# Mixing one chunk of tokens with matrix products, and a new order for the first stage of a banded-attention and gated feed-forward kernel

## The chip, the cores and the metric

The kernel runs on one core of one Trainium2 chip. The metric is device time in microseconds (us), the median over several executions; lower is better. TensorE (PE) does matrix products, with its weight loads (PEld) shown apart; VectorE is DVE, ScalarE is ACT, GpSimd is POOL, and SP is the engine that issues all transfers (DMA).

## The reference

Eight batches, eight heads, 576 tokens, 64 numbers per head, all fp32. Per head, two attentions are added. The pooled one averages q, k and v over groups of four tokens (144 groups), attends over all groups, and repeats each result four times. The local one attends only to tokens less than four away.

```python
out_up = np.repeat(sm_attn(q_d, k_d, v_d), 4, axis=2)      # q_d, k_d, v_d: means over 4 tokens
scores = np.where(np.abs(pos[:, None] - pos[None, :]) < 4, scale * q @ k.T, -1e9)
x = out_up + softmax(scores) @ v                            # heads side by side: (8, 576, 512)
x_prev = x shifted by one token, zeros in front
xk = mu_k * x + (1 - mu_k) * x_prev
xr = mu_r * x + (1 - mu_r) * x_prev
v  = np.maximum(xk @ w_k, 0) ** 2 @ w_v                     # w_k 512x1024, w_v 1024x512
out = sigmoid(xr @ w_r) * v                                 # w_r 512x512
```

The weights w_k, w_v, w_r arrive in double precision.

## The kernel before

**Attention.** Two heads make a pair; a batch has four pairs, and there are 32 of them (`n`). For a pair, q and k are loaded in 128-byte pieces (`load_raw`), turned on VectorE, and pooled on GpSimd. v is loaded twice: pooled groups (`load_v4`) and windows of 32 tokens (`load_windows`). The scores go to PSUM; `score_*` is the local softmax, `down_*` the pooled one. `down_turn` transposes the pooled probabilities with TensorE, in two tiles that share the 144 keys: keys 0 to 111 in one, keys 16 to 143 in the other, of which 80 to 143 are used. `av_pe` multiplies with v. Its pooled product has two halves (64 columns of sums per head, on array rows 0 to 63 and 64 to 127), and the second tile is added in a second step on rows 64 to 127. The result is `xts[b]`, x turned so that features lie on partitions.

**Feed-forward.** The 4608 tokens are cut into 18 chunks of 256 (`c`). Mixing makes xk and xr. Since x*mu + x_prev*(1-mu) is x_prev + mu*(x - x_prev), chunk 0 and 1 take the difference on GpSimd (`diff`), scale it on ScalarE (`mix_part`), and add on VectorE (`mix_add`); `mix_high` rounds to the faster format fp32r, and `mix_low` keeps what is left. Every product is made of three such products: high by high, high by low, low by high. `k_pe` is the first layer, `v_pe` the second, `r_pe` the gate, `store_mul` and `store_out` the end.

**Weights.** Twenty blocks (k0 to k7, v0 to v7, r0 to r3) of 512 KB each. A block is fetched, scaled on ScalarE, put together from its two integer words in three passes on VectorE, and split into high and low parts; the low part of the first eight (in the order of `WORDER`) is made by two products on TensorE (`weight_diff`), of the others by GpSimd. It needs a PSUM bank from its scaling on.

**Order.** All work is written as tasks with an engine, a cost, a rank, and the tiles that they read and write. `Plan.order` places one task after another: the one that can start first on its engine, and among those that can start at that time the one with the lowest rank. This order is fixed for every engine's queue. `SHIFT` is a table of additions to ranks, for tasks of chunks 0 to 3, pairs 0 to 9 and the weights. Six PSUM banks are handed out by the plan, and two more hold scores. Where TensorE would be idle during the first 100 us of the plan, `fill` puts in products whose results nobody reads (`keep_warm`). The lines that the rows name: L281 and L282 load the mixing's coefficients; L320 fetches a weight block; L325 to L360 convert it; L356 is filler; L600 to L602 are `down_turn`; L620, L624 and L630 are `av_pe`; L664 writes x; L685 to L719 are the mixing; L727 is `k_pe` of chunks 0 and 1; L792 is `v_pe`; L796 multiplies by the gate.

Of the kernel before, what the change touches and what calls it, by code (L numbers as in the profile page):

```python
# [16 lines left out]
DM, DFF = 512, 1024  # L17
# [22 lines left out]
KA = 112  # L40
SHIFT = {
# [24 lines left out]
class Plan:  # L66
# [18 lines left out]
    def shift(self, name, args):  # L85
        if not args:
            return SHIFT.get(name, 0.0)
        i, more = args[0], args[1:]
# [166 lines left out]
def attention_moe(ctx: ExitStack, tc, q, k, v, mu_k, mu_r, w_k, w_v, w_r, band, ident, out):  # L255
# [10 lines left out]
    muk = cp.tile([P, NP], F32, name="muk")  # L266
    mur = cp.tile([P, NP], F32, name="mur")
# [34 lines left out]
    raws, ws, shaped, part32 = {}, {}, {}, {}  # L302

# [78 lines left out]
    def load_v4(n):  # L382
        b, p = divmod(n, NP)
        v4 = v4s[n % 2]
        base = (b * H + 2 * p) * S * D
        nc.sync.dma_start(v4[0:KA, 0:2, :], bass.AP(v.tensor, base, [[4 * D, KA], [S * D, 2], [1, 4 * D]]))
        nc.sync.dma_start(v4[96:P, 2:4, :], bass.AP(v.tensor, base + KA * 4 * D, [[4 * D, 32], [S * D, 2], [1, 4 * D]]))
        st.setdefault(n, {})["v4"] = v4
# [200 lines left out]
    def down_turn(n):  # L589

        d = st[n]
        if n < NP:
            d["ps_t"] = [pp.tile([P, 288], F32, tag=plan.bank[f"pst{n}{kt}"], name="ps_t", bufs=1) for kt in range(2)]
        else:
            ps = pp.tile([P, 1024], F32, tag="att", name="ps_t", bufs=1)
            d["ps_t"] = [ps[:, 512 * kt:512 * kt + 288] for kt in range(2)]
        for kt, (ps, ks) in enumerate(zip(d["ps_t"], (slice(0, KA), slice(16, 144)))):
            d["ps_t"][kt] = ps = ps[0:ks.stop - ks.start]
# [6 lines left out]
    def down_copy(n):  # L605
# [3 lines left out]
        nc.scalar.activation(aT[64:P, 1, :], d["ps_t"][1][64:P], AF.Copy)  # L609
# [451 lines left out]
```

## Time and profile before

| | us |
|---|---|
| median of 3 runs | 694.76 (693.29 to 698.73) |
| the profiled execution | 695.45 |
| its span, first to last instruction | 693.7 |

The profile is one execution. Busy shares of its span: TensorE 97%, VectorE 75%, ScalarE 70%, GpSimd 44%. The ends of matrix products are modelled and overlap, so starts tell more than durations: what a product costs in a queue is the distance between starts.

### The profile page before, as it was taken

The numbers are of one execution on the slowest core, as the hardware profiler recorded it, in microseconds if no ns is written. First come the engines' busy times: TensorE is split into PE (matmuls) and PEld (weight loads), VectorE is DVE, ScalarE is ACT, GpSimd is POOL, SyncE is SP. The second block draws the span as 40 slices with busy tenths as digits, with TensorE's granted clock in tenths as the row PEclk, the third lists the DMA queues.
The fourth block names the chain that finished last, engine by engine and source line by source line (L and its number), as shares of the span: only waits on it lengthen the run. The fifth ranks groups of instructions, "written<-read, shape, count | busy, mean of one in ns | idle before, by whom it ended". The sixth has DMA issues, their size and how long they took to land.

```text
span 693.7 us, 18197 instructions
## 1 busy us (share of the span) xinstructions
PE 670.1 (97%) x7084; PEld 558.9 (81%) x7084; DVE 521.2 (75%) x1015; ACT 488.3 (70%) x1223; POOL 305.7 (44%) x376
## 2 busy tenths in 40 slices
PE   7887999999999999999999999999998999999997
PEld 5666787888888888888888887888887888888886
DVE  3989987799879987998475888699849874675322
ACT  3648877688767886877666676788669585855553
POOL 6465799764445454433343355454534431000000
PEclk9999999999999999999999999999999999999999
DMA  9999989753344345142242333533421100000000
GB/s 172 182 185 290 215 137 160 143 104 88 72 114 101 78 104 107 35 105 50 56 107 58 71 85 80 127 65 100 84 65 46 41 3 32 1 30 31 1 31 32
DMA packets 222489, 62.19 MB, mean 90 GB/s; under 512 B 205762, under 2 KB 215234, under 8 KB 222402
## 3 DMA queue, kind: packets, MB, share of 16 engines
q1 hardware_dynamic: 222402, 61.02, 40.9%
q8 instruction: 56, 0.92, 0.6%
q14 instruction: 31, 0.25, 0.1%
HBM read 51.55 MB, written 9.44 MB: 88 GB/s over the span
## 4 chain that ended last, share of the span: by engine, by line
PE 77%; DVE 6%; POOL 5%; DMA 3%; ACT 3%; issue 2%; SPq 2%; DVEq 0%; POOLq 0%; ACTq 0%
PE acc L792 25%; PE ps_g L731 16%; PE ps_r L777 14%; PE ps_g L733 8%; PE ps_v L630 3%; PE ps_a L492 3%; PE ps_v L620 2%; DMA wk<-in_moe_w_k_dram 1%; PE ps_a L559 1%; PE ps_t L600 1%; PE ps_t L602 1%; POOL ad L587 1%; PE ps_a L552 1%; DMA vw<-in_v_dram 1%; SPq L377 1%
## 5 line engine op out<-in xcount | busy, mean ns | idle before, releaser
L792 PE MATMUL acc<-wv,kh 128*128 128x512 f32 x576 | 182.2, 398 | 0.0
L731 PE MATMUL ps_g<-xk,wk 128*128 128x512 f32 x512 | 142.0, 399 | 1.9 <-DVE xk L719 1.8
L792 PEld LDWEIGHTS acc<-wv,kh 128*128 128x128 f32 x576 | 101.8, 190 | 17.7 <-ACT kh L759 0.2
L792 PE MATMUL acc<-wv,kl 128*128 128x512 f32 x288 | 113.5, 394 | 0.4 <-DVE kl L766 0.3
L731 PEld LDWEIGHTS ps_g<-xk,wk 128*128 128x128 f32 x512 | 92.6, 189 | 20.9 <-issue 2.4
L777 PE MATMUL ps_r<-wr,xr 128*128 128x512 f32 x432 | 104.3, 395 | 0.0
L766 DVE TENSOR_TENSOR kl<-kk,kh 128x256 fp32r<-128x256 f32 x119 | 65.5, 551 | 40.0 <-ACT kh L759 38.6
L744 DVE TENSOR_TENSOR kk<-ps_g,kk 128x256 f32<-128x256 f32 x128 | 52.6, 416 | 56.5 <-ACT kk L739 55.9
L777 PEld LDWEIGHTS ps_r<-wr,xr 128*128 128x128 f32 x432 | 79.8, 188 | 17.3
L739 ACT ACTIVATE kk<-ps_g 128x256 f32<-128x256 f32 x128 | 48.0, 381 | 59.8 <-PE ps_g L733 53.6
L733 PEld LDWEIGHTS ps_g<-xk,wk 128*128 128x128 f32 x512 | 79.0, 189 | 11.2
L733 PE MATMUL ps_g<-xk,wk 128*128 128x256 f32 x512 | 81.6, 282 | 0.0
L766 POOL TENSOR_TENSOR kl<-kk,kh 128x256 fp32r<-128x256 f32 x25 | 21.6, 864 | 120.1 <-ACT kh L759 120.0
L753 ACT ACTIVATE kk<-kk 128x256 f32<-128x256 f32 x128 | 52.8, 412 | 28.7 <-DVE kk L744 27.9
L792 PEld LDWEIGHTS acc<-wv,kl 128*128 128x128 f32 x288 | 54.3, 188 | 13.3 <-DVE kl L766 1.2
L759 ACT ACTIVATE kh<-kk 128x256 fp32r<-128x256 f32 x144 | 60.2, 418 | 6.8 <-PE acc L792 2.3
L758 ACT ACTIVATE kk<-kk 128x256 f32<-128x256 f32 x144 | 60.1, 418 | 4.3
L466 POOL TENSOR_TENSOR vd<-v 128x256 f32<-128x256 f32 x32 | 31.5, 985 | 49.5 <-PE ps_v L624 48.1
L520 POOL TENSOR_TENSOR sm<-sm,mx 128x384 f32<-128x384 f32 x28 | 24.0, 857 | 55.6 <-DVE mx L515 35.3
L456 POOL TENSOR_TENSOR tk<-kz 64x288 f32<-64x288 f32 (+1 forms) x56 | 40.9, 730 | 15.2 <-DVE kz L424 6.9
L440 POOL TENSOR_TENSOR tq<-qT 128x288 f32<-128x288 f32 x32 | 21.7, 678 | 57.0 <-DVE qT L415 54.3
L465 POOL TENSOR_TENSOR v<-v 128x512 f32<-128x512 f32 x32 | 45.5, 1421 | 2.6 <-DMA v<-in_v_dram 1.4
(114 smaller groups left out, 1323.6 us busy)
## 6 DMA issues: line engine op xcount, KB each, us to landing
vw<-in_v_dram SPq DMA_DIRECT2D x126, 96.0 KB, 3.2
qraw<-in_q_dram SPq DMA_DIRECT2D x128, 72.0 KB, 2.6
kraw<-in_k_dram SPq DMA_DIRECT2D x128, 72.0 KB, 2.6
out_dram<-sig SPq DMA_DIRECT2D x36, 256.0 KB, 2.2
v<-in_v_dram SPq DMA_DIRECT2D x32, 224.0 KB, 3.2
wv<-in_moe_w_v_dram SPq DMA_DIRECT2D x8, 512.0 KB, 6.0
wk<-in_moe_w_k_dram SPq DMA_DIRECT2D x8, 512.0 KB, 6.6
v<-in_v_dram SPq DMA_DIRECT2D x32, 64.0 KB, 2.9
```

The source lines that it names most:

```text
L456: nc.gpsimd.tensor_tensor(out=tk[h], in0=k4[:, :, 0:2], in1=k4[:, :, 2:4], op=ALU.add)
L465: eng.tensor_tensor(out=v4[:, :, 0:128], in0=v4[:, :, 0:128], in1=v4[:, :, 128:256], op=ALU.add)
L731: nc.tensor.matmul(ps, w_k_part(p, f, 0), x[:, :, p, :], start=(p == 0), stop=False)
L733: nc.tensor.matmul(ps[:, 0], w_k_part(p, f, 1), x[:, 0, p, :], start=False, stop=(p == NP - 1))
L739: nc.scalar.activation(kk, ps[:, 1], AF.Copy)
L744: nc.vector.tensor_tensor(out=kk, in0=ps[:, 0], in1=kk, op=ALU.add)
L753: nc.scalar.activation(kq[c, f], kq[c, f], AF.Relu)
L758: nc.scalar.activation(kk, kk, AF.Square)
L759: nc.scalar.activation(kh, kk, AF.Copy)
L766: eng.tensor_tensor(out=kl, in0=kk, in1=kh.bitcast(F32), op=ALU.subtract)
L777: nc.tensor.matmul(ps, x[:, y, p, P * t:P * t + P], ws[f"r{p}"][:, w, :], start=(m == 0), stop=(m == len(mm) - 1))
L792: nc.tensor.matmul(accs[c][t], x[:, P * t:P * t + P], ws[f"v{f}"][:, w, :], start=(f == 0 and m == 0), stop=(f == NF - 1 and m == 2))
```

## The change

1. Chunk 0's mixing goes to TensorE. Diagonal matrices with mu and with 1 - mu are made once, by scaling the identity. Per group of 128 features, two fp32 products, one with x and one with x_prev, are summed in PSUM. ScalarE rounds a copy of the sum to fp32r, VectorE keeps the rest. Each group can start when its pair's x is there. The other chunks mix as before.
2. The coefficients are loaded as rows and turned by TensorE, in place of being loaded in 4-byte pieces.
3. The pooled keys are split at 32: the first tile holds keys 32 to 143, the second has keys 0 to 71, of which 0 to 63 are used, with the second step of the pooled product on rows 0 to 63, into the first half's sum.
4. The last chunk's second block of tokens finishes its last unit in two halves of 256 columns, each multiplied and stored by itself.
5. `SHIFT` is another table; a few costs that the plan uses differ by 0.01 to 0.02 us.

```diff
+MU = -95.0
 SHIFT = {
...
+    "fetch_weight.2": -6.9, "fetch_weight.3": 2.9, "fetch_weight.5": 54.5, "fetch_weight.6": 48.1,
+    "fetch_weight.7": 84.1, "fetch_weight.8": 5, "k_high.0.2": -16.7, "k_high.3.3": 3.3, "k_low.2.0": 24.8,
...
+    "k_low.2.1": 7, "k_low.2.7": -37.9, "k_low.3": -27.5, "k_low.3.4": -5.1, "k_low.3.7": 71.1, "k_pe.0": -57.4,
...
     def load_mus():
-        nc.sync.dma_start(muk, mu_k.rearrange("(p r) -> r p", r=P))
-        nc.sync.dma_start(mur, mu_r.rearrange("(p r) -> r p", r=P))
+        rows = bd.rearrange("p a c -> p (a c)")
+        nc.sync.dma_start(rows[0:NP, 0:P], mu_k.rearrange("(p r) -> p r", r=P))
+        nc.sync.dma_start(rows[NP:2 * NP, 0:P], mu_r.rearrange("(p r) -> p r", r=P))
...
+    def diagonals(nm):
+        diags[nm] = wp.tile([P, NP, 2, P], F32, tag="f32tmp", name="diag", bufs=2)
+        a = 0 if nm == "xk" else 1
+        for p in range(NP):
+            for j in range(2):
+                nc.scalar.activation(diags[nm][:, p, j, :], idn, AF.Copy, scale=mus[:, a + 2 * j, p:p + 1])
...
-        for kt, (ps, ks) in enumerate(zip(d["ps_t"], (slice(0, KA), slice(16, 144)))):
-            d["ps_t"][kt] = ps = ps[0:ks.stop - ks.start]
+            d["ps_t"] = [ps[0:m, 512 * kt:512 * kt + 288] for kt, m in enumerate((KA, 72))]
+        for ps, ks in zip(d["ps_t"], (slice(32, 144), slice(0, 72))):
...
-        h = slice(64, P)
+        h = slice(0, 64)
         for e in range(2):
-            nc.tensor.matmul(pv[1][64 * e:64 * e + 64, up], d["vd"][h, 2 + e, :], aT[h, 1, 144 * e:144 * e + 144],
+            nc.tensor.matmul(pv[0][64 * e:64 * e + 64, up], d["vd"][h, 2 + e, :], aT[h, 1, 144 * e:144 * e + 144],
                              start=False, stop=True)
...
+    def mix_pe(c, nm, p):
+        m = mixes.setdefault(c, {})
+        if p % 2 == 0:
+            m[nm, p] = pp.tile([P, 2, CT], F32, tag=plan.bank[f"mx{nm}{p}"], name="ps_m", bufs=1)
+        ps = m[nm, p - p % 2]
+        for j in range(2):
+            nc.tensor.matmul(ps[:, p % 2, :], diags[nm][:, p, j, :], xts[0][:, p, 1 - j:1 - j + CT],
+                             start=(j == 0), stop=(j == 1))
...
         for t in range(2):
...
+            for h in columns(c, t) if f == NF - 1 else columns(0, 0):
+                for m, (x, w) in enumerate(((kh, 0), (kh, 1), (kl, 0))):
...
+        if c == 0:
+            for nm in ("xk", "xr"):
+                for p in range(NP):
+                    u, R = [f"mx{nm}{p - p % 2}"], X - 20 + p + (0 if nm == "xk" else 8)
+                    add("PE", 1.1, R, mix_pe, c, nm, p, r=[("xt0", p), f"diag{nm}"],
+                        new=[(u[0], "bank")] if p % 2 == 0 else [], w=u if p % 2 else [])
+                    add("ACT", 0.36, R, mix_split, c, nm, p, r=u, new=[(f"{nm}0", nm)] if p == 0 else [],
+                        w=[(f"{nm}0", 0, p)])
+                    add("DVE", 0.36, R, mix_rest, c, nm, p, r=u + [(f"{nm}0", 0, p)], w=[(f"{nm}0", 1, p)])
```

Of the new ranks on SP's queue, worked out from the table and the base ranks: the coefficients -95; weight blocks k0 -93.5, k1 -93, k3 -88.2, v0 -81, v5 -66.2, k5 -59, k2 -57, k4 -55, k6 -51.9, k7 -49.6, v2 -32.7, v1 -18.7, v3 3.4; the inputs q and k of pairs 0, 1 and 2 at -92.8, -90 and -69.4; the windows of pairs 0, 1 and 2 at -87.8, -70.2 and -64.4. Before, v1 stood at -107.9, k0 at -93.5, k1 at -93, k2 at -88.6, k3 at -88.5, v2 at -84.1, v0 at -58.6, and the inputs of pair 0 at -94.

## Rows read from the trace of the kernel before

**Rows 1.** Busy us (and instructions) by stage: stretch, length, engines, granted clock, DMA share, GB/s.

```profile
0.00:59.85 59.85, 48.41 (x808) 35.57 (x808) 43.04 (x87) 31.66 (x82) 33.06 (x56) 1.00 0.97 194
59.85:71.63 11.78, 11.25 (x41) 8.23 (x41) 11.05 (x17) 9.68 (x19) 7.44 (x6) 0.86 1.05 277
71.63:80.16 8.53, 8.17 (x156) 7.31 (x156) 8.18 (x14) 6.75 (x17) 5.56 (x7) 1.00 0.88 182
80.16:114.34 34.18, 31.60 (x475) 26.74 (x472) 28.64 (x50) 27.28 (x67) 32.96 (x37) 1.00 0.97 164
...
140.00:689.93 549.93, 545.88 (x5192) 458.70 (x5190) 409.84 (x813) 394.70 (x986) 206.30 (x248) 1.00 0.29 65
```

**Rows 2.** The same stretches for the filler tile alone: PE, PEld, clock, DMA.

```profile
0.00:59.85 59.85, 21.84 (x78) 15.92 (x78) 1.00 0.97 194
59.85:71.63 11.78, 9.36 (x36) 7.05 (x36) 0.86 1.05 277
```

**Rows 3.** Timeline of TensorE: start, us, engine, line, operation, count, idle before.

```profile
58.01 0.83 PE L620 MATMUL ps_v<-adT,vd 64*64 64x144 f32 x8 [1.83 <-DVE xt L664]
...
71.63 5.68 PE L727 MATMUL ps_g<-xk,wk 128*128 128x256 f32 x47 [0.53 <-DVE xk L719]
...
80.16 0.73 PE L792 MATMUL acc<-wv,kh 128*128 128x512 f32 x2
```

**Rows 4.** Timelines of VectorE and GpSimd around chunk 0's mixing.

```profile
61.73 0.82 DVE L664 TENSOR_TENSOR xt<-ps_v,up 128x288 f32<-128x288 f32 x2
...
66.83 1.24 DVE L710 TENSOR_TENSOR xk<-xk,xt 128x1024 f32<-128x1024 f32 x1
...
69.53 2.04 DVE L719 TENSOR_TENSOR xk<-xk,xk 128x1024 fp32r<-128x1024 f32 x1
...
62.64 1.90 POOL L685 TENSOR_TENSOR dx<-xt 128x1024 f32<-128x1024 f32 x1 [1.72 <-DVE xt L664]
```

**Rows 5.** Timeline of TensorE, one weight block's two products and what follows.

```profile
28.87 1.13 PE L349 MATMUL ps_w<-w,idn 128*128 128x512 f32 x2 [0.47 <-DVE w L338]
...
30.16 0.29 PE L600 MATMUL ps_t<-idn,ad 128*112 128x128 f32 x1
```

**Rows 6.** Groups by line and shape: busy us, mean ns of one, idle before and releasers.

```profile
L750 ACT ACTIVATE kk<-ps_g 128x256 f32<-128x256 f32 x16 | 5.9, 374 | 1.9 <-PE ps_g L727 1.4 <-POOL kl L766 0.4
L744 DVE TENSOR_TENSOR kk<-ps_g,kk 128x256 f32<-128x256 f32 x128 | 52.6, 416 | 56.5 <-ACT kk L739 55.9
```

**Rows 7.** Transfers by line with us to landing, and SP's timeline (first and tenth fetch).

```profile
muk<-in_moe_mu_k_dram SPq DMA_DIRECT2D x1, 2.0 KB, 6.4
...
1.65 0.42 SPq L320 DMA_DIRECT2D wv<-in_moe_w_v_dram  x1
...
22.33 0.43 SPq L281 DMA_DIRECT2D muk<-in_moe_mu_k_dram  x1
...
50.45 0.42 SPq L320 DMA_DIRECT2D wv<-in_moe_w_v_dram  x1
```

**Rows 8.** Groups by line, VectorE, 29.88 to 62.55 us: the first of a block's three passes.

```profile
L329 DVE TENSOR_SCALAR ps_w<-ps_w 128x512 int32<-128x512 int32 x8 | 5.5, 691 | 2.5 <-ACT ps_w L325 2.5
```

**Rows 9.** Timeline of TensorE, one pair's transposes and the product behind them.

```profile
182.21 0.27 PE L600 MATMUL ps_t<-idn,ad 128*112 128x128 f32 x1
...
182.56 0.31 PE L600 MATMUL ps_t<-idn,ad 128*128 128x128 f32 x1
...
182.95 1.17 PE L731 MATMUL ps_g<-xk,wk 128*128 128x512 f32 x4
```

**Rows 10.** Timeline of TensorE, one pair's second pooled part (L624) and windows (L630).

```profile
49.72 0.21 PE L630 MATMUL ps_v<-bd,vw 64*64 64x48 f32 x2
49.73 0.29 PE L624 MATMUL ps_v<-adT,vd 64*64 64x144 f32 x2
...
49.88 0.95 PE L630 MATMUL ps_v<-bd,vw 64*64 64x48 f32 x42
```

**Rows 11.** Timeline of VectorE, the last two multiplications.

```profile
689.29 1.37 DVE L796 TENSOR_TENSOR sig<-acc,sig 128x512 f32<-128x512 f32 x2 [0.77 <-PE acc L792]
```

More of the change, by code (lines that the diff above doesn't have):

```diff
@@ L265, in attention_moe @@
     nidn = cp.tile([P, P], F32R, name="nidn")
[L266 to L267 removed]
+    mus = cp.tile([P, 4, NP], F32, name="mus")
+    muk, mur = mus[:, 0, :], mus[:, 1, :]
     qds = [cp.tile([P, 272], F32, name=f"qd{i}") for i in range(2)]
@@ L712, in mix_high @@
     def mix_high(c, nm):
-        x = wp.tile([P, 2, NP, CT], F32R, tag=nm, name=nm, bufs=2 if nm == "xk" else 1)
+        x = mixed(nm)
         nc.scalar.activation(x[:, 0], mixes[c][nm], AF.Copy)
@@ L790, in v_pe, with columns, store_mul, store_out @@
         for t in range(2):
-            for m, (x, w) in enumerate(((kh, 0), (kh, 1), (kl, 0))):
-                nc.tensor.matmul(accs[c][t], x[:, P * t:P * t + P], ws[f"v{f}"][:, w, :],
-                                 start=(f == 0 and m == 0), stop=(f == NF - 1 and m == 2))
-    def store_mul(c, t):
-        nc.vector.tensor_tensor(out=gates[c][t], in0=accs[c][t], in1=gates[c][t], op=ALU.mult)
-    def store_out(c, t):
-        r0 = c * CT + P * t
-        nc.sync.dma_start(outf[r0:r0 + P, :], gates[c][t])
+            for h in columns(c, t) if f == NF - 1 else columns(0, 0):
+                for m, (x, w) in enumerate(((kh, 0), (kh, 1), (kl, 0))):
+                    nc.tensor.matmul(accs[c][t][:, h], x[:, P * t:P * t + P], ws[f"v{f}"][:, w, h],
+                                     start=(f == 0 and m == 0), stop=(f == NF - 1 and m == 2),
+                                     skip_group_check=(h.start > 0))
+    def columns(c, t):
+        n = 2 if (c, t) == (NCH - 1, 1) else 1
+        return [slice(DM // n * i, DM // n * (i + 1)) for i in range(n)]
+    def store_mul(c, t, i):
+        h = columns(c, t)[i]
+        nc.vector.tensor_tensor(out=gates[c][t][:, h], in0=accs[c][t][:, h], in1=gates[c][t][:, h], op=ALU.mult)
+    def store_out(c, t, i):
+        r0, h = c * CT + P * t, columns(c, t)[i]
+        nc.sync.dma_start(outf[r0:r0 + P, h], gates[c][t][:, h])
     plan = Plan(dict(raw=4, vw=3, kd=2, sm=2, ad=1, adT=1, at=1, up=2, vd=2, xt=2, f32tmp=2, xk=2,
@@ L910, in chunk, with parts_of, places @@
             add("DVE", 1.22, X + o + 4, mix_low, c, nm, r=[src], w=[f"{nm}{c}"])
+    def parts_of(nm, c):
+        return [f"{nm}{c}"] + ([(f"{nm}0", y, p) for y in range(2) for p in range(NP)] if c == 0 else [])
+    def places(c, T):
         where = {}
@@ L923, in chunk @@
                     held.pop(0)()
-            add("PE", 1.43 if c < WIDE else 1.38, W, k_pe, c, f, r=[f"xk{c}"] + both(f"k{4 * (f // 4) + p}" for p in range(NP)),
+            add("PE", 1.43 if c < WIDE else 1.40, W, k_pe, c, f, r=parts_of("xk", c) + both(f"k{4 * (f // 4) + p}" for p in range(NP)),
                 new=[(f"g{c}.{f}", "bank")])
@@ L937, in r_part @@
                 add("PE", 2.79, where[f"r{t}"], r_pe, c, t,
-                    r=[f"xr{c}"] + both(f"r{p}" for p in range(NP)), new=[(f"r{c}.{t}", "bank")])
+                    r=parts_of("xr", c) + both(f"r{p}" for p in range(NP)), new=[(f"r{c}.{t}", "bank")])
             add("ACT", 3.8, where["r1"] - 3, gate, c, r=[f"r{c}.0", f"r{c}.1"],
@@ L949, in s_part @@
             for t in range(2):
-                add("DVE", 0.67, where["v7"] - 6, store_mul, c, t, r=[f"acc{c}.{t}"], w=[f"sig{c}.{t}"])
+                n = len(columns(c, t))
+                for i in range(n):
+                    add("DVE", 0.67 / n, where["v7"] - 6, store_mul, c, t, i, r=[f"acc{c}.{t}"],
+                        w=[f"sig{c}.{t}"] if n == 1 else [(f"sig{c}.{t}", i)])
             for t in range(2):
-                add("SP", 0.5, where["v7"] + 4, store_out, c, t, r=[f"sig{c}.{t}"], dma=0.9)
+                n = len(columns(c, t))
+                for i in range(n):
+                    add("SP", 0.5, where["v7"] + 4, store_out, c, t, i,
+                        r=[f"sig{c}.{t}"] if n == 1 else [(f"sig{c}.{t}", i)], dma=0.9 / n)
         if c == 0:
@@ L966, in begin_all @@
         add("POOL", 4.2, -110, clear, w=["kT0", "kT1", "qT0", "qT1", "qd.0", "qd.1", "bd"])
-        add("SP", 1.0, -88.0, load_mus, w=["mu"], dma=0.8)
+        add("SP", 1.0, MU, load_mus, w=["bd"], dma=0.1)
+        add("PE", 0.15, MU, turn_mus, r=["bd", "idn"], new=[("mus", "bank")])
+        add("ACT", 0.5, MU, copy_mus, r=["mus"], w=["mu"])
+        for nm in ("xk", "xr"):
+            add("ACT", 2.0, MU + 20, diagonals, nm, r=["mu", "idn"], new=[(f"diag{nm}", "f32tmp")])
     begin_all()
```

40 lines of the change are left out of this document (32 added, 8 removed), and 30 rows, old and new, of the table SHIFT.

## The prediction

> **What bounds the kernel now.** The busy time by stage comes first, because the shares of the whole span hide everything here [rows 1]. From 140 us until the last matmul at 689.93 us TensorE is busy for 545.9 of 549.9 us at full clock; nothing there waits long, and only fewer or cheaper matmuls can shorten it. Before 80 us it looks busy as well, and that is the trap: the view of the filler tile shows that 31 us of it (21.8 and 9.4, up to 71.63 us) are matmuls that only keep the clock up [rows 2]. So the time before is one stretch of some 80 us that waits for other engines and for transfers, and behind it a stretch in which TensorE has real work without a pause. The end moves by as much as the dense stretch begins earlier, plus what its own matmuls change.
>
> Next the timeline of TensorE [rows 3]: the first batch's last product with v begins at 58.01 us, chunk 0's first layer runs from 71.63 us, and its second layer from 80.16 us. What lies between the first two is read in the rows of VectorE, GpSimd and ScalarE: the last quarter of x is written at 61.73 + 0.82 = 62.55 us, GpSimd takes the difference until 64.54, ScalarE scales, VectorE adds (66.83), and the low part is only there after the 2.04 us that begin at 69.53 [rows 4]. That is 71.63 - 62.55 = 9.1 us in which TensorE has nothing but filler. The other engines are close to full as well: VectorE 11.05 of 11.78 us between 59.85 and 71.63, GpSimd 32.96 of 34.18 us between 80.16 and 114.34, and the DMA share is 0.88 to 1.05 in all four stretches up to 114.34 [rows 1]. Whatever starts earlier runs into these.
>
> **Chunk 0's mixing.** Removed: one difference on GpSimd (1.90), eight scalings, two roundings, two additions (1.24 for the one in the rows) and two low parts (2.04) [rows 4]. Added on TensorE are eight sums of two fp32 products of 256 columns. One fp32 and one fp32r product of 512 columns took 30.16 - 28.87 = 1.29 us together [rows 5]; two fp32r ones of that width show 0.73 us [rows 3], so an fp32 one of 512 columns costs 0.92 to 1.29 us, a sum of two of 256 the same, and I take 1.1: 8.8 us in all. Per sum ScalarE copies 256 columns (0.37) and VectorE subtracts (0.42) [rows 6]. Six sums belong to pairs whose x is written before the last one's, and are due early enough to take the place of filler; xk's last lies on the path, and of xr's four I let 0.5 us reach the dense stretch (0 to 4.4, if all four do). The sixteen scaled identities cost ScalarE at most 16 x 0.37 = 6 us; before 59.85 us it is busy for 31.66 us [rows 1], and that idle time hides them; without it the 6 us would stand ahead of ScalarE's work on the pairs.
>
> The new chain is 1.1 + 0.37 + 0.42 and three hand-overs of some 0.09 (the distance from 62.55 to 62.64 in [rows 4]): 2.2 us in place of 9.1, so **6.9 us** at most. What is late next? Everything up to 114.34 us would have to come as much earlier. Between 71.63 and 114.34 (42.7 us) GpSimd works 38.5, VectorE 36.8, and the DMA rings, by their shares, 7.5 + 33.2 = 40.7 us [rows 1]: free are 4.2, 5.9 and 2.0 us, and the change gives GpSimd 1.9 and VectorE some 3 us for xk alone. So DMA lets 2.0 us through if its order stayed, the chain 6.9; I take the middle, **-4.5** (0 to -6.9).
>
> The coefficients came in as two transfers of 4-byte pieces, issued at 22 us; the one that the trace follows needed 6.4 us to land [rows 7]. Now they are four rows each, ahead of the pairs' loads on SP's queue (rank -95), with 0.43 us per issue in front of every later load; a product and two short copies follow. I put this at nothing between -1 and +0.9.
>
> **The order of the first stage.** By the ranks in the diff, SP now fetches two weight blocks (k0, k1 at -93.5 and -93) ahead of pair 0's inputs (-92.8); before it was one (1.65 us) [rows 7]. Pair 0 can so be 512 KB later: 2.7 us at the 194 GB/s of this stretch [rows 1]. On the other hand ten weight blocks went out ahead of the last pair's windows, the first at 1.65 and the tenth at 50.45 us [rows 7]; by the new ranks it is about six (k0, k1, k3, v0, v5, k5), since k2, v1, v2 and v3 are put off. Four blocks less are 10.8 us of transfer. But k2 is needed for the first layer too, and comes behind k5, which takes back 5.4. And each block put off costs VectorE three passes of 0.69 us [rows 8] in a stretch where it has little room: up to 8.2 us for four. So the bounds are -8 (most of 10.8) and +6 (8.2 less what VectorE has free); half of 10.8 - 5.4 seems likely, **-2.5**.
>
> **The keys split at 32.** The second transposed tile has 72 columns instead of 128. In steady state the first tile (112 columns) takes 182.56 - 182.21 = 0.35 us and the second 182.95 - 182.56 = 0.39 [rows 9]. In it the two transposes move 128 columns whichever the width, so I let only the first and the two narrow products gain: 0.06 us per pair, and 28 pairs lie in the dense stretch: **-1.7** (0, to 0.04 x 56/16 x 28 = -3.9 if all loads set the pace). The Trainium skill ("TensorE: Matmul & The Clock Gate", LDWEIGHTS) has a load cost its columns divided by 1.2 ns, that is 47 ns less for each of four loads, by its figures an estimated 5.2 us for the 28 pairs, and 683.1 in the sum; the 0.04 us for 16 columns fit that, but not which of the steps they lie in.
>
> The pooled product's second part moves from array rows 64 to 127 to rows 0 to 63, into the sum of the other half. Before, the windows' first product (rows 0 to 63) starts at 49.72 us, ahead of the second part's at 49.73, though it is queued behind it [rows 10]: the halves run side by side, and I take 0. The bound is one of the windows' six steps (0.95/6 = 0.16 us) left uncovered in 28 pairs: 0 to +4.5; the mirrored gain is bounded by the same. The skill (same page, Part 3, The mechanism) says that products start and end strictly in queue order; then the second part would cover nothing in its new place and the sum would be 691.1. The row with 49.72 speaks against it here.
>
> **The last unit in halves.** The multiplications of the last chunk take 1.37 us for two [rows 11]. Now they are 0.68 and twice about 0.42 [rows 6], in one queue: the last ends some 0.1 us later, and its store is half as large. Zero, within 0.3.
>
> **The sum.** -4.5 - 2.5 - 1.7 + 0.5 = -8.2. The profiled execution has 695.45 us (693.7 span and 1.75 around it), which gives 687.25; it lies 0.69 above the median of 694.76, so I predict **686.6 us**. A measurement of this kernel can tell about 1% (6.9 us) from no change.
>
> **Rivals.** (1) *Given back.* GpSimd and the DMA rings are full up to 114 us, and TensorE idles there for what it gained: the chain keeps 2, the order nothing: 694.8 - 2 - 1.7 + 0.5 = 691.6. For it speaks 32.96 of 34.18 us; against it the work that the change takes from GpSimd and VectorE. (2) *The weights end last.* The new mixing isn't what the first layer waits for, since k2 comes late: from landing to its low part a block needs three passes of 0.69 [rows 8], 1.29 for the two products [rows 5] and three copies of up to 0.74 (twice 256 columns [rows 6]), 5.6 us, so it must land by 59.1 for a start at 64.7. If it lands at 64, the start is 69.6: the chain keeps 2.0 and the order nothing: 691.6. That would be a change that doesn't do what it says. (3) *Transfers decide.* The fewer blocks ahead of the pairs' loads count nearly in full: -5 - 8 - 1.7 + 0.5 gives 680.6. The DMA share of 0.97 before 59.85 us speaks for it, VectorE's 8.2 us against it. (4) *All loads set the pace of the transposes:* -3.9 in place of -1.7, 684.4. (5) *The second part in queue order:* +4.5, 691.1. (6) *Banks, slower.* The sums of the mixing hold two of six PSUM banks from the first pair's x until the second's, then two more; a pooled product and a transpose take two each, and the weights' conversion needs one at a time. Between 29.88 and 62.55, from about there to the last pair's x, eight blocks were converted [rows 8]. Each one pushed behind the mixing costs 2.05 us of VectorE there. Three cancel the other terms; from seven on (14.4 - 5.7) it is slower by over 1%, about 703.
>
> **How the numbers follow.** The forecast, 683 to 690, has 0.36; rivals 1 to 6 have 0.14, 0.06, 0.15, 0.10, 0.08 and 0.11. Left out of 678 to 697 are the sixth and about half of the third, 0.18. Faster by over 1% (below 687.8): 0.6 of the forecast, the third and the fourth, 0.47, rounded to 0.48. Slower (over 701.7): the sixth, 0.11. Within: 0.41. The likeliest case's own range is 683 to 690.
>
> **What would show it.** The first row of chunk 0's first layer some 2.2 us behind the last row that writes x, and filler before it cut by about as much as the start moved; no wait there for a weight; GpSimd's and TensorE's idle time between 80 and 140 not above 6 us more than now; a second tile of the transposes at 0.33 us; the windows' first product still beginning beside the second part of the pooled one. The prediction is wrong if the first layer begins by 65 us and the dense stretch doesn't, or if x itself is written much earlier or later than 62.55.

## The result and the profile after

The changed kernel takes **689.94 us** (median of 8 runs, 688.36 to 691.82). The kernel before took 697.77 beside it (8 runs, 693.29 to 699.82). The ratio is 0.9905, with a 95% interval of 0.9883 to 0.9926: some 6.6 us faster, just within the 1% that the prediction counted as no change. (The two medians lie 7.8 us apart; the text goes by the ratio and its interval.) The forecast was 686.6, the range 678 to 697, and of the three outcomes the prediction held faster by over 1% for the likeliest (0.48, against 0.41 for this one). The profiled execution took 690.9 us with a span of 689.1; before it was 695.45 and 693.7.

The first view is the timeline of all engines of the changed kernel around chunk 0's first layer, which answers to [rows 3, 4]: start, us, engine, line, operation, count, idle before. L688 writes x, L734 is a mixing sum, L740 and L744 split it, L773 is the first layer.

```profile
59.72 0.82 DVE L688 TENSOR_TENSOR xt<-ps_v,up 128x288 f32<-128x288 f32 x2
60.59 2.00 PE L734 MATMUL ps_m<-xt,diag 128*128 128x256 f32 x8 [0.31 <-DVE xt L688]
60.62 1.20 ACT L350 ACTIVATE ps_w<-wk 128x512 f32<-128x512 f32 x2 [1.03 <-DVE xt L688]
...
61.76 0.57 ACT L385 ACTIVATE wk<-ps_w 128x512 fp32r<-128x512 f32 x1
...
62.24 0.36 ACT L740 ACTIVATE xk<-ps_m 128x256 fp32r<-128x256 f32 x1
...
62.51 0.70 DVE L358 SCALAR_TENSOR_TENSOR ps_w<-wk,ps_w 128x512 int32<-128x512 int32 x1
...
63.11 0.42 DVE L744 TENSOR_TENSOR xk<-ps_m,xk 128x256 fp32r<-128x256 f32 x1
...
63.58 1.09 PE L773 MATMUL ps_g<-xk,wk 128*128 128x256 f32 x7 [0.99 <-DVE xk L744]
```

From the last x (60.54) to the first layer (63.58) it is now 3.04 us; before it was 9.1 [rows 3, 4]. x itself comes 2.0 us earlier. What is left of the chain is not mixing alone: ScalarE has weight work (L350, L385) in its queue ahead of the copy, and VectorE's weight passes (the last of them L358 at 62.51) stand ahead of the subtraction. The first layer waits for xk and for no weight. All in all it starts 8.05 us earlier.

A sum of two products is cheaper than forecast. In the timeline of TensorE two sums lie between the starts 39.36 and 41.00, 0.82 us each. That is below the 0.92 to 1.29 that the prediction had worked out.

```profile
39.36 1.99 PE L734 MATMUL ps_m<-xt,diag 128*128 128x256 f32 x8
41.00 1.27 PE L381 MATMUL ps_x<-nidn 128*128 128x512 f32 x4
```

Busy time by stretch of the changed kernel, which answers to [rows 1] (stretch, length, PE, PEld, DVE, ACT, POOL, granted clock, DMA share, GB/s):

```profile
0.00:63.58 63.58, 50.19 (x816) 36.56 (x816) 44.61 (x95) 38.22 (x108) 34.65 (x56) 0.97 0.97 197
63.58:70.48 6.90, 6.90 (x52) 6.38 (x53) 6.63 (x11) 6.37 (x16) 5.29 (x8) 1.00 0.95 153
70.48:114.34 43.86, 40.60 (x612) 33.55 (x611) 35.99 (x61) 34.15 (x86) 36.12 (x42) 0.96 1.03 191
114.34:200.00 85.66, 83.06 (x1021) 70.70 (x1020) 71.75 (x148) 62.17 (x167) 45.61 (x61) 1.00 0.51 111
...
200.00:689.10 489.10, 481.91 (x4575) 404.05 (x4574) 355.46 (x708) 343.00 (x866) 177.04 (x212) 1.00 0.28 63
```

The filler tile alone in the changed kernel, which answers to [rows 2]:

```profile
0.00:63.58 63.58, 16.63 (x55) 11.39 (x55) 0.97 0.97 197
63.58:200.00 136.42, 2.43 (x10) 1.88 (x10) 0.99 0.70 139
```

The kernel before, cut at its own start of the first layer:

```profile
0.00:71.63 71.63, 59.65 (x847) 43.80 (x848) 54.09 (x103) 41.34 (x101) 40.51 (x61) 0.98 0.98 208
71.63:200.00 128.37, 124.58 (x1665) 107.09 (x1666) 111.58 (x207) 98.63 (x256) 90.78 (x107) 1.00 0.66 128
200.00:693.70 493.70, 485.88 (x4574) 408.00 (x4572) 355.49 (x706) 348.38 (x868) 174.43 (x208) 1.00 0.27 62
```

These three fences give an account of the 4.6 us between the two spans, at a mean granted clock of 0.995 in both. TensorE's real work ahead of the first layer was 59.65 - 31.20 = 28.45 us (the filler is 21.84 + 9.36 [rows 2]) and is now 50.19 - 16.63 = 33.56: the four pairs of sums came in (1.97, 1.99, 1.98 and 2.00 us, 7.9 in all), so 2.8 us of other work moved behind the first layer. Idle and filler time behind it was 3.79 + 0.85 + 7.82 = 12.46 us (0.85 of filler up to 200 us) and is now 0 + 3.26 + 2.60 + 2.43 + 7.19 = 15.48. Real work behind it stayed the same (609.61 and 610.04 us) although 2.8 us were moved there, so its own matmuls shrank by 2.4. The sum: the start gives 8.05, the moved work takes 2.8, new idle time 3.0, and cheaper matmuls give 2.4. Over all executions the mean granted clock is 0.998 in the changed kernel and 0.991 to 0.992 in the kernel before (beside the runs below), so what 6.6 us hold beyond the 4.6 may lie in the clock; no run holds the clock fixed.

The waits of TensorE behind the first layer, up to 200 us (line waited for, in total, times, longest), show where the new idle time lies. First the changed kernel:

```profile
PE ps_a L522 <- issue: 1.6, 1, 1.6
PE ps_g L777 <- DVE xk L765: 1.6, 1, 1.6
...
PE acc L839 <- ACT wv L385: 0.8, 1, 0.8
PE ps_t L624 <- POOL ad L612: 0.8, 1, 0.8
```

And the kernel before:

```profile
PE ps_a L497 <- issue: 1.5, 1, 1.5
PE ps_a L552 <- POOL kd L457: 1.5, 2, 1.1
```

New are a wait for VectorE (xk of a later chunk), one for ScalarE (a weight block) and one for GpSimd (a pair's probabilities), besides 2.43 us of filler in place of 0.85; that for a pair's pooled keys (kd) fell from 1.5 to 0.5. The wait that no releaser in the profile ends ("issue") is not new: before it was as long. What differs behind it is the clock. In the changed kernel the twelve products that follow take 2.23 us, while other groups of twelve take 1.57 to 1.68, and the granted clock is 0.96 from 70.48 to 114.34; before it is 1.00 from 71.63 to 114.34 [rows 1].

```profile
98.63 0.32 PE L522 MATMUL ps_a<-kz,qT 64*32 64x32 f32 x21 [1.60 <-issue]
98.88 2.23 PE L773 MATMUL ps_g<-xk,wk 128*128 128x256 f32 x12
```

The steady state shows the keys. One pair's transposes in the changed kernel, which answer to [rows 9]: the second tile takes 186.68 - 186.36 = 0.32 us, before 0.39. The first takes 0.39 here, behind a wait, and 0.34 at 216.78, much as before (0.35).

```profile
185.97 0.32 PE L624 MATMUL ps_t<-idn,ad 128*112 128x128 f32 x1 [0.81 <-POOL ad L612]
...
186.36 0.28 PE L624 MATMUL ps_t<-idn,ad 128*72 128x128 f32 x1
...
186.68 0.70 PE L839 MATMUL acc<-wv,kh 128*128 128x512 f32 x2
```

And the pooled product's second part, which answers to [rows 10]. It now starts at 206.30, ahead of the windows (206.31), no longer behind them; but from the first score product (L577) to the first of the local scores (L517) it is 1.92 us:

```profile
205.67 0.41 PE L577 MATMUL ps_a<-kd,qd 128*128 128x144 f32 x2
...
206.30 0.29 PE L648 MATMUL ps_v<-adT,vd 64*64 64x144 f32 x2
206.31 0.32 PE L654 MATMUL ps_v<-bd,vw 64*64 64x48 f32 x4
...
207.59 0.88 PE L517 MATMUL ps_a<-kz,qT 128*32 128x64 f32 x48
```

In the kernel before the same steps lie at 203.39 and 205.32, 1.93 us apart.

The end, which answers to [rows 11]: the last three multiplications start at 684.75 and the three stores follow at 685.47. From the start of the last product (685.14, 0.28 us) to the end of the span it is 3.96 us.

```profile
684.75 1.47 DVE L849 TENSOR_TENSOR sig<-acc,sig 128x512 f32<-128x512 f32 x3 [0.84 <-PE acc L839]
...
685.14 0.28 PE L839 MATMUL acc<-wv,kl 128*128 128x256 f32 x1
685.47 1.31 SPq L853 DMA_DIRECT2D out_dram<-sig  x3
```

### The profile page after: what moved, and what is told of

It reads as the page before. It is cut to its first block, busy times and chain, and to the rows that moved or that the text cites. A ratio compares the mean times of both kernels' runs of the same rounds, so it can differ in the third digit from the quotient of the medians.

```text
span 689.1 us, 18215 instructions
## 1 busy us (share of the span) xinstructions
PE 662.7 (96%) x7070; PEld 551.2 (80%) x7070; DVE 514.4 (75%) x1020; ACT 483.9 (70%) x1239; POOL 298.7 (43%) x375
## 4 chain that ended last, share of the span: by engine, by line
PE 73%; DVE 13%; ACT 5%; SPq 3%; issue 2%; DMA 2%; POOL 2%; DVEq 0%; ACTq 0%; POOLq 0%
PE acc L839 23%; PE ps_g L777 14%; PE ps_r L823 13%; PE ps_g L779 7%; PE ps_v L654 3%; PE ps_a L517 3%; SPq L402 2%; PE ps_g L773 2%; PE ps_v L644 2%; ACT L601 1%; POOL ad L612 1%; DMA wv<-in_moe_w_v_dram 1%; ACT ad L601 1%; PE ps_a L584 1%; PE ps_a L577 1%
## 5 line engine op out<-in xcount | busy, mean ns | idle before, releaser
L839 PEld LDWEIGHTS acc<-wv,kh 128*128 128x128 f32 x578 | 102.3, 189 | 18.7 <-ACT wv L385 1.1
L790 DVE TENSOR_TENSOR kk<-ps_g,kk 128x256 f32<-128x256 f32 x128 | 52.4, 415 | 51.9 <-ACT kk L785 51.5
L812 DVE TENSOR_TENSOR kl<-kk,kh 128x256 fp32r<-128x256 f32 x119 | 63.4, 533 | 36.5 <-ACT kh L805 35.4
L481 POOL TENSOR_TENSOR tk<-kz 64x288 f32<-64x288 f32 (+1 forms) x56 | 42.8, 765 | 18.7 <-DVE kz L454 8.8
L491 POOL TENSOR_TENSOR vd<-v 128x256 f32<-128x256 f32 x32 | 27.8, 870 | 50.0 <-PE ps_v L648 48.5
L490 POOL TENSOR_TENSOR v<-v 128x512 f32<-128x512 f32 x32 | 43.7, 1365 | 5.0 <-DMA v<-in_v_dram 4.6
L591 DVE TENSOR_REDUCE mxd<-ps_a 128x3 f32<-128x432 f32 x32 | 19.3, 602 | 34.3 <-PE ps_a L517 29.1
```

What stands on the lines that cost most here:

```text
L481: nc.gpsimd.tensor_tensor(out=tk[h], in0=k4[:, :, 0:2], in1=k4[:, :, 2:4], op=ALU.add)
L490: eng.tensor_tensor(out=v4[:, :, 0:128], in0=v4[:, :, 0:128], in1=v4[:, :, 128:256], op=ALU.add)
L790: nc.vector.tensor_tensor(out=kk, in0=ps[:, 0], in1=kk, op=ALU.add)
L812: eng.tensor_tensor(out=kl, in0=kk, in1=kh.bitcast(F32), op=ALU.subtract)
L839: nc.tensor.matmul(accs[c][t][:, h], x[:, P * t:P * t + P], ws[f"v{f}"][:, w, h], start=(f == 0 and m == 0), stop=(f == NF - 1 and m == 2) ...
```

## The experiments

The first theory was the prediction's: each part has a price of its own, and the prices add up. The rival was that the parts only make sense together, above all the mixing and the order, since the sums need PSUM banks that the old order has no room for. Each run is compared with the kernel before on the same chip: its median was 696.62 us beside runs 1 to 4, 696.50 beside 5 to 8, and 696.42 beside 9 to 12.

**1. The keys alone**, in the kernel before.

```diff
-        for kt, (ps, ks) in enumerate(zip(d["ps_t"], (slice(0, KA), slice(16, 144)))):
+        for ps, ks in zip(d["ps_t"], (slice(32, 144), slice(0, 72))):
```

> The kernel before with the keys split at 32 alone. The theory: only the first transpose and the narrow products of the second tile get cheaper, 0.06 us in each of the 28 pairs of the dense stretch: 1.7 us faster, the second tile's step 0.33 us instead of 0.39. Rival, all loads set the pace: 3.9 to 5.2 us faster, the step at 0.25. Rival, the second part waits in the queue: 0.16 us more per pair, together 2.8 us slower or no change, with no product with the windows starting beside the second part.

Measured: 692.79 us, ratio 0.9950 (0.9935 to 0.9965), 2.4 to 4.5 us faster, between the theory's 1.7 and the rival's 3.9 to 5.2. The term of -1.7 is too small. The rows show 0.07 us per pair in the second tile, 2.0 us for 28 pairs and 2.2 for all 32; the profiled span fell by 1.3. The mean granted clock of the executions was 0.9937, and 0.9916 in those of the kernel before beside them; by an estimate, 0.0021 of 695 us, at most 1.5 us of the 3.5 lie in that. Whether the keys raise the clock or it was chance, no run shows.

**2. The order alone**: the new `SHIFT` and costs in the kernel before.

```diff
 SHIFT = {
...
+    "fetch_weight.2": -6.9, "fetch_weight.3": 2.9, "fetch_weight.5": 54.5, "fetch_weight.6": 48.1,
+    "fetch_weight.7": 84.1, "fetch_weight.8": 5, "k_high.0.2": -16.7, "k_high.3.3": 3.3, "k_low.2.0": 24.8,
...
```

> The kernel before with the new table of ranks and the plan's new costs, and nothing else of the change: chunk 0 mixes as before. The theory: fewer weight blocks ahead of the pairs' loads bring the last x about 2 us earlier, and the end moves by 2.5 us at most, since the blocks put off are converted in the stretch where VectorE and GpSimd are full. Rival, the order is the whole change: 5 us faster or more. Rival, the table fits only the new mixing: slower than before by up to 5 us.

Measured: 720.46 us, ratio 1.0347 (1.0328 to 1.0365), 24 us slower, far outside all three readings. The waits of TensorE from 60 to 200 us (line waited for, in total, times, longest) show what ends last: xk, for the first layers of the first chunks. That is not the price of the new order itself: run 9 keeps the changed kernel's order with the old mixing in it and is 2.9 us faster than before. The 24 us belong to the plan that is made anew from this table with the old steps.

```profile
PE ps_g L734 <- DVE xk L722: 6.4, 1, 6.4
PE ps_t L603 <- POOL tk L459: 3.4, 1, 3.4
...
```

**3. The mixing alone**: TensorE's mixing and the coefficients as rows in the kernel before, with the old table. The planner here also waits for both buffers of a step that takes two of a kind; run 12 has that alone.

```diff
+        if c == 0:
...
+                    add("PE", 1.1, R, mix_pe, c, nm, p, r=[("xt0", p), f"diag{nm}"],
+                        new=[(u[0], "bank")] if p % 2 == 0 else [], w=u if p % 2 else [])
```

> The kernel before with chunk 0's mixing by TensorE and the coefficients loaded as rows, under the old table of ranks; two chunks' gate tiles are also counted singly in the plan, which changes the order from about chunk 2 on. The theory: the chain from the last x to the first layer falls from 9.1 to about 3 us, and 4.5 us of the 6 arrive at the end. Rival, given back: the first layer starts 6 us earlier, but the end moves by less than 2 us. Rival, weights: the first layer itself starts less than 3 us earlier.

Measured: 730.11 us, ratio 1.0483 (1.0459 to 1.0506), 34 us slower, which none of the three readings had. The waits from 30 to 100 us look like the rival with the banks: TensorE waits for weights that stand behind others in VectorE's queue, and so do the pooled products.

```profile
PE ps_w L371 <- DVE w L360: 10.3, 5, 5.7
PE ps_v L642 <- DVE w L360: 3.0, 2, 1.9
```

The x of pairs 1 to 3 is written at 70.88, 76.08 and 80.31 us, before at 54.52, 57.41 and 61.73; the first layer starts at 84.12. The stretches of this run show a second loss, that of the granted clock: 0.59 from 60 to 80 us, where TensorE is busy for 14.93 of 20 us, and 0.93 between 200 and 300, where it is busy for 88.18 of 100.

```profile
60.00:80.00 20.00, 14.93 (x203) 11.29 (x203) 10.24 (x20) 10.56 (x25) 6.50 (x8) 0.59 0.96 204
```

**4. Mixing and order together**, without the keys and the halves of the last unit.

```diff
-        for ps, ks in zip(d["ps_t"], (slice(32, 144), slice(0, 72))):
+        for kt, (ps, ks) in enumerate(zip(d["ps_t"], (slice(0, KA), slice(16, 144)))):
-        n = 2 if (c, t) == (NCH - 1, 1) else 1
+        n = 1
```

> The changed kernel without the keys split and with the last unit whole: mixing by TensorE and the new order together. The theory: the two add up, 6 to 7 us faster than before, and the keys' 1.7 us are all that is missing. If the order is only worth something with the mixing, this run gains clearly more than the runs with either alone do together.

Measured: 692.67 us, ratio 0.9947 (0.9923 to 0.9970), 3.7 us faster. +24 and +34 make -3.7: the additive theory falls. With the keys' -3.5 it makes -7.2, the whole change within the intervals, so that nothing is left for the halves of the last unit.

**5. Run 3 with a bank for each sum.**

```diff
-        if p % 2 == 0:
-            m[nm, p] = pp.tile([P, 2, CT], F32, tag=plan.bank[f"mx{nm}{p}"], name="ps_m", bufs=1)
-        ps = m[nm, p - p % 2]
+        m[nm, p] = ps = pp.tile([P, CT], F32, tag=plan.bank[f"mx{nm}{p}"], name="ps_m", bufs=1)
```

> The third run (mixing by TensorE in the old order) with one thing changed: each of chunk 0's mixing sums stands in a PSUM bank of its own, given back when the copy and the addition of its own feature pair are done, instead of a bank shared by two pairs. If the third run's 33.6 us are the banks held from the first pair's sum to the second's (the rival with the banks), the x of pairs 1 to 3 comes out earlier than 70.88, 76.08 and 80.31, the first layer starts some 10 us or more before that run's 84.12, and the time falls by at least 10 us, to under 720. If it is the order of the work around the sums (weights and pooled products pushed behind whatever the banks do), the first layer stays within 4 us of 84 and the time stays between 722 and 736.

Measured: 727.62 us, ratio 1.0449 (1.0409 to 1.0488). Half of each reading came: the first layer starts at 72.45, 12 us earlier, which fits banks that held it up, though the plan behind it is another as well; but the time falls by only 2.5. Most of the loss isn't there. TensorE is busy for 12.30 of 20 us between 160 and 180 and for 90.94 of 100 between 200 and 300, far behind the mixing. The planner, given other tasks with the same table, puts the later ones into another order; that this is the loss is argued, not tested.

**6. The changed kernel with a bank for each sum**, planned anew, with the planner's alteration of runs 3 and 5 (run 12) in it as well.

```diff
-                        new=[(u[0], "bank")] if p % 2 == 0 else [], w=u if p % 2 else [])
+                        new=[(u[0], "bank")])
```

> The changed kernel with the same alteration: each mixing sum in a bank of its own. In its order the two sums of a bank are made one behind the other (39.36 to 41.00 us for two), so that sharing costs little: the theory that its order has taken the banks out of the way expects 686 to 694, within 0.5% of the changed kernel's 689.9. If the shared banks still hold up its first stage, the time falls by 2 us or more and the first layer starts before 63.6.

Measured: 708.55 us, ratio 1.0181 (1.0155 to 1.0206): 18.6 us slower than the changed kernel, a miss for both. The first layer starts at 62.91, earlier than the changed kernel's; the loss lies at 140 to 160 us (TensorE 12.22 of 20) and at 200 to 300 (96.54 of 100). An edit that takes a constraint away comes out 19 us slower, with another plan behind it: VectorE's queue has another order from 74 us on. How much of it is the planner's alteration was not tried in the changed kernel. So a comparison in which the planner runs anew can't price an edit here, runs 2, 3, 5 and 6 included; runs 9 and 10 hold the order.

**7 and 8. More work for VectorE, and for GpSimd**, in the changed kernel's own order. One pass over each weight block is made twice on VectorE (20 of 0.69 us more), or GpSimd's subtraction for the low parts (12 of 1.30 more).

```diff
+        nc.vector.scalar_tensor_tensor(out=wi, in0=raws[i][:, :, 0], scalar=29, in1=wi,
+                                       op0=ALU.logical_shift_right, op1=ALU.bitwise_or)
```

```diff
+        eng.tensor_tensor(out=lo, in0=part32[i], in1=hi.bitcast(F32), op=ALU.subtract)
```

> The changed kernel with one pass of VectorE over each weight block done twice (the same bits are set again, the result is the same): some 20 passes of about 0.69 us more, 14 us in all, nearly all of it before 200 us. If VectorE is the engine that gives back half of the earlier first layer (it is busy for 19.3 of 20 us between 60 and 80), most of it reaches the end: 699 to 706. If the transfers set the pace of the weights' stretch, at most a third: 690 to 695. If GpSimd does, as little.

> The changed kernel with GpSimd's subtraction for the low parts of the weights done twice: some 12 passes of about 1.3 us more, 16 us in all. If GpSimd sets the pace of the weights' stretch, 700 to 708; if VectorE does, at most a quarter of it reaches the end, 690 to 694; if the transfers do, none, 688 to 691.

Measured: 699.99 us, ratio 1.0058 (1.0032 to 1.0084), for VectorE, and 697.02, ratio 1.0014 (0.9999 to 1.0030), for GpSimd. Against the changed kernel's 689.94 that is 10.1 of 13.9 added us (0.73) and 7.1 of 15.6 (0.45). With VectorE's passes the first layer moves to 69.46. GpSimd's don't touch it (62.38), and what they cost comes later. Run 7 lies at the lower end of what was expected if VectorE gives back half of the earlier start (699 to 706); run 8 lies between its readings (690 to 694, and 700 to 708).

**9. The changed kernel with the old mixing, its order held.** Chunk 0 is mixed by GpSimd, ScalarE and VectorE, and the coefficients are loaded as before; each engine's other instructions keep the changed kernel's order, and so do the banks.

```diff
+            k = key_of(t)
+            if k in known and FORCED[t["eng"]][place[t["eng"]]] != k:
+                return None
+            if k in banked and FORCED["banks"][place["banks"]] != k:
+                return None
```

> The changed kernel with chunk 0's mixing made by GpSimd, ScalarE and VectorE as before, and every other instruction held in the changed kernel's own order on its engine and in its order of taking banks (the mixing's instructions are put in where they can start). Nothing is planned anew, so the difference to the changed kernel is the mixing itself. If TensorE's mixing is worth the chain that it shortens, and half of that is given back as in the first layer's 8 us, the first layer starts some 6 us later than 63.6 and the time is 692 to 695; if it is worth the whole, 696 to 698; if nothing (all of it is given back, and the 24 us that the new order alone lost were the old steps in the wrong places), 688 to 691.

Measured: 693.52 us, ratio 0.9956 (0.9937 to 0.9974), 3.6 us over the changed kernel. The chain is back, from 62.07 to 69.66, 7.6 us:

```profile
61.25 0.82 DVE L711 TENSOR_TENSOR xt<-ps_v,up 128x288 f32<-128x288 f32 x2
...
69.66 4.42 PE L796 MATMUL ps_g<-xk,wk 128*128 128x256 f32 x35 [0.66 <-DVE xk L788]
```

So TensorE's mixing, with its identities and its way of loading the coefficients, is worth 3.6 us in this order (some 1.6 to 5.6, by the intervals of the two ratios). In the profiled execution the first layer is 6.1 us later; but that execution is the slowest of its run (697.29 us, the median is 693.52), and it holds a wait of 3.66 us before the last x that nothing in the profile ends:

```profile
53.94 2.29 PE L404 MATMUL ps_x<-nidn 128*128 128x512 f32 x5 [3.66 <-issue]
```

What share of a later first layer reaches the end can't be read from it. The new order with the old mixing, keys split, is 2.9 us faster than before, which the keys' 3.5 account for: the order by itself gives nothing that shows.

**10. The kernel before with the new mixing, its order held** in the same way, a bank for each sum.

```diff
+                    add("PE", 1.1, R, mix_pe, c, nm, p, r=[("xt0", p), f"diag{nm}"],
+                        new=[(u[0], "bank")])
...
+            if k in known and FORCED[t["eng"]][place[t["eng"]]] != k:
+                return None
```

> The kernel before with chunk 0's mixing by TensorE, each sum in a bank of its own, and every other instruction held in the order of before. If the shorter chain is worth something by itself, the first layer starts 4 to 7 us before 71.6 and the time falls to 690 to 694. If the banks that the sums take hold the pooled products and the weights of that order up, the last x comes out later than 62.6 by as much as the chain is shorter, the first layer starts between 69 and 73, and the time is 695 to 702. If the third run's 33.6 us belong to the mixing in any order, some 730.

Measured: 700.02 us, ratio 1.0055 (1.0033 to 1.0076), 3.6 us slower than before. The time, the last x (66.10 + 0.82, 4.4 us later than before) and the first layer (71.56, as before) lie where the reading with the banks has them, but the trace shows another cause. ScalarE makes the sixteen scaled identities in one piece, ahead of a weight block's scaling (22.04, before 16.86) and of a pair's exponentials (22.59, before 18.18):

```profile
17.36 4.78 ACT L327 ACTIVATE diag<-idn,mus 128x128 f32<-128x128 f32 x16
22.04 0.64 ACT L371 ACTIVATE ps_w<-wk 128x512 f32<-128x512 f32 x1
22.59 0.53 ACT L570 ACTIVATE sm<-sm 128x384 f32<-128x384 f32 x1
...
57.87 0.82 DVE L710 TENSOR_TENSOR xt<-ps_v,up 128x288 f32<-128x288 f32 x2
...
66.10 0.82 DVE L710 TENSOR_TENSOR xt<-ps_v,up 128x288 f32<-128x288 f32 x2
68.32 2.00 PE L754 MATMUL ps_m<-xt,diag 128*128 128x256 f32 x8
```

The kernel before, the same two steps:

```profile
16.86 0.63 ACT L325 ACTIVATE ps_w<-wk 128x512 f32<-128x512 f32 x1
18.18 0.52 ACT L524 ACTIVATE sm<-sm 128x384 f32<-128x384 f32 x1 [0.69 <-DVE sm L510]
```

The pairs behind stay late: x of pair 0 comes 2.9 us later (31.97, before 29.06), that of pairs 1 and 2 by 3.3 us (57.87 and 60.74), and that of the last by 4.4. From 17 us to the first layer no instruction outside the mixing waits for a step of it, so no row shows that its banks hold the pairs up; ScalarE stands for 3.0 us more in front of the copies, until their sums are there. In the changed kernel the identities stand ahead of a pair's exponentials too, but there they cost next to nothing: these start at 19.13, and at 19.02 in run 9, which has no identities and waits for VectorE.

```profile
14.43 4.79 ACT L306 ACTIVATE diag<-idn,mus 128x128 f32<-128x128 f32 x16
19.13 0.51 ACT L549 ACTIVATE sm<-sm 128x384 f32<-128x384 f32 x1
```

What the shorter chain gains, the later x takes. The 3.6 us are lost behind the first layer: TensorE is busy for 36.74 of the 42.78 us from 71.56 to 114.34, at a granted clock of 0.92, and before for 39.77 of 42.71, at 1.00. The mixing is worth -3.6 us in the new order and costs 3.6 in the old one. No run made the identities elsewhere, or gave the old order more banks.

**11. Less work for VectorE**: the pass that run 7 doubles is left out, so the three lowest bits of each weight block are missing.

```diff
     def weight_tail(i):
         wi = shaped[i].bitcast(I32)
-        nc.vector.scalar_tensor_tensor(out=wi, in0=raws[i][:, :, 0], scalar=29, in1=wi,
-                                       op0=ALU.logical_shift_right, op1=ALU.bitwise_or)
+        return
```

> The changed kernel without VectorE's pass that sets the three lowest bits of each weight block (20 passes, 13.7 us; the weights are then off in those bits), in the same order. If VectorE gives the weights' stretch its pace, as 10 of 14 added microseconds reaching the end say, taking the passes away gives back a like share: 680 to 684. If another engine or the transfers are due right behind it, at most a quarter: 686 to 689.

Measured: 688.83 us, ratio 0.9901 (0.9872 to 0.9930), beside the changed kernel's 0.9905. Taking 13.7 us from VectorE gives nothing that shows, though giving it as much costs 10. The first layer starts at 60.87, 2.7 us earlier, and idle and filler time from there to 200 us is 139.13 - 131.38 + 2.43 = 10.2 us, against 8.3 in the changed kernel. The waits of TensorE from 20 to 200 us say who is late next; those for GpSimd's kd and sm are 1.1 us each in the changed kernel:

```profile
PE ps_a L576 <- POOL kd L481: 2.6, 3, 1.9
PE ps_a L576 <- POOL sm L559: 2.2, 2, 1.1
...
PE ps_v L643 <- ACT wk L384: 1.4, 1, 1.4
```

**12. The planner's alteration of run 3 alone**, in the kernel before.

```diff
-                old = ring[tag][0]
-                if old is not None:
+                for old in ring[tag][:same]:
```

> The kernel before with the one alteration of the planner that the third run (TensorE's mixing in the old order) also had: a step that takes two buffers of one kind is planned for when both are free, not the first alone. The order of the instructions changes from about chunk 2 on. If that alteration is a part of that run's 33.6 us, the time rises by several microseconds; if not, it stays within 2 us of before, 694 to 698.

Measured: 694.33 us, ratio 0.9973 (0.9957 to 0.9989). It is no part of run 3's loss; by itself it gives some 1.9 us.

## Why the prediction was right, and where it was not

**The size.** -6.6 us were measured, -8.2 forecast, on an execution that lies close to the median. The sum held, with three of its terms moved, and in part that is luck: the order was put 2.5 us too high and the keys 1.8 too low, and the two nearly cancel.

**The chain** (2.2 us long by the forecast, 3.04 measured; worth -4.5 + 0.5 by the forecast, -3.6 in run 9). Right in mechanism and nearly in size. The sums were dearer in the forecast (1.1, measured 0.82); what it left out is that the copy and the subtraction stand in queues behind weight work. It put the sixteen identities (4.8 us measured) into ScalarE's idle time; in the new order that came true, in the old one (run 10) they stood ahead of the pairs' work, as the prediction had said they would without that idle time. Taking the middle between what the chain gives and what the engines let through came near: of 8.05 us, 2.8 went to work moved behind the first layer and 3.0 to new idle time, so by this account 2.2 reach the end, and by run 9 it is 3.6 (1.6 to 5.6). The forecast named GpSimd and the DMA rings as what is late next, with VectorE third. The waits behind the first layer and runs 7, 8 and 11 say that it is no single one: more work costs time on VectorE and on GpSimd (ScalarE was not tried), and relief for VectorE alone gives none that shows, as TensorE then waits for GpSimd and ScalarE (run 11). How much the transfers do was not tried; their share is 1.03 from 70.48 to 114.34.

**The order** (-2.5). This step failed. It took the order as a term of its own, priced by the weight blocks that leave the queue ahead of the last pair's loads. The count was right: six blocks go out ahead of the last pair's windows, before it was ten. x does come 2.0 us earlier, but with the old mixing in place it is worth nothing beyond the keys (run 9), and planned anew without the mixing it loses 24 us (run 2). Its worth is that the mixing finds its place in it, as far as the traces show on ScalarE: 3.6 us lost in the old order (run 10) become 3.6 gained.

**The keys** (-1.7, measured -3.5, between -2.4 and -4.5). The term was too small, and its upper bound of -3.9 was the better guess. Rows support 0.07 us per pair, not 0.06, and that is 2.0 to 2.2 us; the rest is in part the clock, by the estimate at run 1, and stays open. The Trainium skill ("TensorE: Matmul & The Clock Gate", LDWEIGHTS) has a load cost in proportion to its columns. The trace agrees in the direction, 0.39 to 0.32 us for 128 to 72 columns; by its figures the forecast had an estimated 5.2 us for the 28 pairs, more than the interval holds.

**The pooled part** (0, measured 1.92 against 1.93 us). Right. The rival in which products go strictly in queue order would have cost 0.16 us per pair; nothing of it shows.

**Coefficients and tail** (0 each). The two loads of coefficients now go out at 9.33 and 9.82 us, and the diagonals are ready before the first sum. From the last product's end to the end of the span it is 3.68 us, before 3.77 (693.70 - 689.93), within the 0.3 allowed.

**The rivals.** The one with the banks, slower, has runs 3 and 5 for it: with a bank for each sum the first layer starts 12 us earlier, but the plan is another too. In run 10, whose sums have banks of their own, x comes late behind the identities (by 2.9 to 3.3 of the 4.4 us), and no pair waits for a sum. In the new order the x of pair 1 follows that of pair 0 by 5.7 us (31.91 and 37.61), so that a shared bank is given back soon, where in the order of before it is 25 us (29.06 and 54.52) and in run 3 37.5 us (33.34 and 70.88). Its condition, that blocks are pushed behind the mixing, is what the order decides, and a queue that has not been seen yet can't be read from the trace of before. "Given back" (691.6) is the rival that came true in most: it let the chain keep 2 us, and the order nothing. The account gives the first 2.2 us and run 9 the second; with the 3.5 measured for the keys its sum is 689.8. That it is GpSimd and the transfers that take the lead back isn't shown: the waits behind the first layer name VectorE, ScalarE and GpSimd. The weights didn't end last, and the transfers didn't give 680.6.

**The signs named beforehand.** The filler before the first layer fell from 31.2 to 16.6 us, more than the start moved, since the sums took its place too. The first layer's first product waits for no weight. TensorE's idle time between 80 and 140 us didn't grow (3.4 before, 2.8 now, filler counted as busy), but GpSimd's did, from 6.5 to 13.5, just over the 6 us that were allowed: it lost work, and it waits more. Of the two signs of being wrong, the first layer did begin by 65 us, and the stretch behind it is dense up to 70.48 (6.90 of 6.90 us) and has gaps after; x was written 2.0 us earlier than 62.55, which the order's term had allowed for. The second tile takes 0.32 us (0.33 forecast). The windows no longer start ahead of the second part, but right with it.

## What to carry to other kernels

Where a planner with a hand-fitted table orders the work, an edit can't be priced by planning anew without it: here a few microseconds of mechanism were hidden under 24 and 34 us of order. Hold the queues and the banks of one version and exchange the edit alone, in both versions: the two differences (here -3.6 and +3.6) show both the price and the interplay. Then read in the trace where the edit's smallest pieces land: here sixteen identities on an engine that is idle for nearly half of the stretch cost nothing in one order and held up the pairs in the other. Before counting a shorter chain in full, list which other engines are within a few per cent of full in the stretch that it runs into; with several of them, 2 to 4 of 8 us came through here.

## What the runs showed of the hardware

The granted clock fell in other places than before (0.86 between 59.85 and 71.63, on filler [rows 1, 2]): to 0.91 between 40 and 60 us, around a wait of 1.92 us that ends at 45.11, and to 0.92 between 100 and 120, on real work, behind a wait of 1.60 us. Filler was 1.72 us between 20 and 40 us (before 6.56) and 5.01 between 40 and 60 (before 4.59). Executions of the changed kernel with a granted clock of 1.000 took 688.4 to 689.9 us, those at 0.995 and 0.998 took 690.0 to 691.8. In run 3 the clock was 0.59 for 20 us in which TensorE was busy for 14.93.

The wait of 1.60 us "for nothing" in the middle of 96 small score products (L522, [1.60 <-issue], with 21 products left) comes back at the same step in runs 4, 7, 8 and 11 (2.04, 1.53, 0.90 and 1.58 us). In the kernel before there is one of 1.48 us at 95.03, with 2 of the 96 left, and in run 9 one of 1.45 us at 119.76, also with 2 left. What it waits for stays open.
